# First layer's weights in three transfers, tails turned by four full transposes: a change at the two ends of a tuned kernel

## The chip, the cores and the metric

The kernel runs on one NeuronCore of a Trainium2 chip. The metric is device microseconds of one execution (lower is better). The time counted is about 1.8 us longer than the span that the profile shows.

Words used below: TensorE does the matmuls, and also turns (transposes) blocks, by a matmul with a unit matrix. Its results go to a buffer, PSUM, of which this kernel uses eight parts, the banks. ScalarE and VectorE copy them out, multiply and add. A transfer is issued by an engine's queue, is then carried out by the DMA engines, and has landed when its semaphore says so.

## The reference, cut to what matters

```python
B, F, D, L = 16384, 26, 16, 6            # Din = F * D = 416
def reference(x0, ws, bs):               # x0 [16384, 416], ws [6, 416, 416], bs [6, 416], bf16
    x = x0
    for l in range(L):
        proj = jnp.einsum('bd,de->be', x, ws[l]) + bs[l]
        x = x0 * proj + x
    return x
```

416 columns are three full tiles of 128 and a tail of 32. The kernel keeps the activations transposed (features on partitions) and cuts the batch into eight groups of 2048 rows, each of four chunks of 512.

## The kernel before: the parts that the change and the argument touch

The program records operations with what they read and write, and puts semaphore waits between them. Each `lane` is a semaphore of a transfer. The start of the SP queue (the SyncE queue that issues transfers), in program order:

```python
def load_wm(l, eng):                      # three full tiles of a layer's weights: one transfer, 312 KB
    add(eng, lambda h: h.dma_start(wm[l][:, :, :], ws[l, 0:NT * P, :].rearrange("(t p) f -> p t f", p=P)),
        writes=[("wm", l)], lane=f"wm{l}", batch=0)
...
load_nat(0, 0, 2); load_nat(0, 2, KK)     # group 0, chunk 0, row-major, 208 KB each
load_wm(0, "sp")
for j in range(1, NJ):                    # chunks 1 to 3
    load_nat(j, 0, 2); load_nat(j, 2, KK)
load_w3(0, "sp")                          # weights of the tail: four small transfers
load_group(1)                             # four DMA transposes of group 1, then four copies of its tails
```

Group 0 is turned by TensorE, group 1 by the DMA engines. `load_group` issues the transposes of tile 0, of the block that holds the tail, of tile 1 and of tile 2, and then the four tail copies.

The last layer of the last group is computed row-major, so that its result can be stored as it is. For that its input has to be turned: tiles 0 and 1 by DMA transposes, tile 2 and the tails by TensorE.

```python
def turn_tails(bks):                      # before: sixteen 32x32 transposes into four banks, one copy
    for kk in range(KK):
        for j in range(NJ):
            r, q = quad(g, l, j)
            add("pe", lambda h, ...: h.matmul(psum_t(b)[:, kk * T32:(kk + 1) * T32], x3col(j, kk), ident[q, q],
                is_transpose=True, tile_position=(r * T32, 0)), ..., writes=[("ps", bks[j])])
    add("act", lambda h: h.activation(x5n[:, :, :, NT * P:D], ..., ACT_F.Copy), reads=[("ps", b) for b in bks] + ...)
...
# rest_turn(1): issues on the SP queue, with a store between the two halves
#   transpose of chunks 0, 1 -> x5n ; store of part of the group before ; transpose of chunks 2, 3 -> x5n
# then, on VectorE:  nat_mul(0, 0), nat_mul(0, 2), nat_add(0, 0), nat_add(0, 2), nat_mul(1, 0) ...
```

`nat_add(0, 2)` is the first operation that needs the second half of that transpose.

## Time and profile before

| | kernel before |
|---|---|
| time, median of six runs | 476.96 us (476.26 to 477.49) |
| span of the profiled execution | 476.1 us |
| TensorE busy | 467.7 us, 98% |
| tail copies of group 1 landed and TensorE goes on | at 22.89 us |
| from there to the issue of the last transpose (460.91) | 438.02 us |
| that transpose, issue to landing | 5.35 us |

The profiled execution itself took 477.91 us. TensorE's timeline of the kernel before (start, length, engine, line, what, and in brackets the idle time and what ended it):

```profile
460.08 0.19 PE L850 MATMUL ps<-ident,x 32*128 32x32 bf16 x3
460.45 0.26 PE L850 MATMUL ps<-ident,x 32*128 32x32 bf16 x13 [0.17 <-ACT tw L395]
...
461.42 0.62 PE L832 MATMUL ps<-ident,x 128*128 128x128 bf16 x8 [0.35 <-ACT x L857]
```

The first two lines are the sixteen small transposes, split by a wait for ScalarE to leave the last of the four banks; the third is the turn of tile 2 (L832), which then waits until ScalarE has copied the tails out.

### The profile page before, as it was taken

What the parts mean: (1) busy time and instruction counts of PE and PEld (TensorE: products, weight loads), DVE (VectorE), ACT (ScalarE), POOL (GpSimd) and SP (SyncE); (2) the same over time, 40 slices, a digit from 0 to 9 for tenths busy, and PEclk for the clock granted to TensorE, in tenths of its full rate; (3) what the DMA queues carried; (4) which work ended last, traced back from release to release, by engine and by line L of the source; (5) the groups of instructions that cost most, each with busy time, mean ns of one, the idle gap of its engine ahead of it and who ended that gap; (6) DMA issues with size and microseconds to landing.
All of it is one profiled execution on the core that took longest, in us unless ns stands there. A gap on an engine that the chain in (4) does not pass through costs nothing.

```text
span 476.1 us, 8364 instructions
## 1 busy us (share of the span) xinstructions
PE 467.7 (98%) x3356; PEld 193.4 (41%) x3356; DVE 403.3 (85%) x695; ACT 341.7 (72%) x371; POOL 5.8 (1%) x15
## 2 busy tenths in 40 slices
PE   8899999999999999999999999999999999999995
PEld 5344444444444444444444444444444444444342
DVE  2788888888888888898889879888888888888886
ACT  4577777777777777777777777777777777777785
POOL 1000000000000000000000000000000000000000
PEclk9999999999999999999999999999999999999999
DMA  8966860630102397369318941980000039025898
GB/s 223 161 163 150 174 122 1 144 79 0 30 7 43 64 224 154 81 143 246 77 25 195 220 95 26 175 264 0 2 12 23 8 64 240 12 45 122 226 192 247
DMA packets 138859, 53.31 MB, mean 112 GB/s; under 512 B 112442, under 2 KB 138308, under 8 KB 138820
## 3 DMA queue, kind: packets, MB, share of 16 engines
q1 hardware_dynamic: 138664, 52.67, 49.6%
q8 instruction: 26, 0.43, 0.4%
q10 hardware_dynamic: 156, 0.11, 0.1%
q14 instruction: 13, 0.11, 0.1%
HBM read 5.97 MB, written 13.63 MB: 41 GB/s over the span
## 4 chain that ended last, share of the span: by engine, by line
PE 90%; SPq 4%; DVE 3%; DMA 2%; ACT 0%; issue 0%; DVEq 0%
PE ps L457 75%; PE ps L478 7%; PE ps L498 7%; SPq L292 2%; DMA x<-x 1%; PE ps L472 1%; DVE x L887 1%; SPq L522 1%; DVE x L881 1%; DVE x L409 1%; DVE tw L404 1%; PE ps L489 1%; SPq L297 0%; ACT tw L395 0%; DMA x<-ost 0%; SPq L303 0%
## 5 line engine op out<-in xcount | busy, mean ns | idle before, releaser
L395 ACT ACTIVATE tw<-ps,bias 128x1024 bf16<-128x1024 f32 (+1 forms) x295 | 299.6, 1070 | 121.4 <-PE ps L478 82.2
L457 PE MATMUL ps<-x,wm 128*128 128x512 bf16 x1692 | 379.6, 380 | 1.3 <-DMA x<-in_x_dram 0.8
L457 PEld LDWEIGHTS ps<-x,wm 128*128 128x128 bf16 x1692 | 158.7, 98 | 215.3 <-issue 28.2
L404 DVE TENSOR_TENSOR tw<-tw,x 128x1024 bf16<-128x1024 bf16 (+1 forms) x285 | 192.8, 684 | 55.6 <-ACT tw L395 55.2
L409 DVE TENSOR_TENSOR x<-tw,x 128x1024 bf16<-128x1024 bf16 (+1 forms) x285 | 182.5, 681 | 0.0
L478 PE MATMUL ps<-x,w 32*128 32x512 bf16 x512 | 39.2, 379 | 0.8 <-DMA x<-ost 0.8
L498 PE MATMUL ps<-x,wm 128*32 128x512 bf16 x564 | 33.0, 380 | 0.0
L435 ACT ACTIVATE ts<-ps,bias 128x512 bf16<-128x512 f32 x47 | 28.7, 700 | 0.0
L498 PEld LDWEIGHTS ps<-x,wm 128*32 128x32 bf16 x564 | 13.8, 96 | 17.6 <-issue 5.3
L439 DVE TENSOR_TENSOR x<-ts,x 128x512 bf16<-128x512 bf16 x47 | 18.6, 418 | 2.4 <-DMA x<-x 2.4
L478 PEld LDWEIGHTS ps<-x,w 32*128 32x128 bf16 x512 | 7.8, 92 | 28.5 <-issue 27.1
L437 DVE TENSOR_TENSOR ts<-ts,x 128x512 bf16<-128x512 bf16 x47 | 18.6, 418 | 0.0
L821 PE MATMUL ps<-wm,x 128*128 128x416 bf16 x48 | 9.5, 340 | 0.0
L684 POOL COPY ost<-ot 128x512 bf16<-128x512 bf16 x6 | 4.3, 720 | 423.7 <-DMA ot<-x 423.7
L875 ACT ACTIVATE x<-ps 128x416 bf16<-128x416 f32 x16 | 7.7, 534 | 2.0 <-PE ps L821 1.9
L575 DVE COPY x<-ps 128x512 bf16<-128x512 bf16 x5 | 2.0, 422 | 8.2 <-PE ps L565 8.1
L577 ACT ACTIVATE x<-ps 128x512 bf16<-128x512 bf16 x7 | 3.8, 595 | 4.9 <-PE ps L565 4.9
L821 PEld LDWEIGHTS ps<-wm,x 128*128 128x128 bf16 x48 | 4.3, 98 | 4.2 <-issue 1.0
L887 DVE TENSOR_TENSOR x<-x,x 128x832 bf16<-128x832 bf16 (+1 forms) x9 | 4.8, 542 | 1.4 <-DMA x<-x 1.3
L489 PE MATMUL ps<-x,w 32*32 32x512 bf16 x188 | 5.9, 374 | 0.0
L472 PE MATMUL ps<-x,w 32*32 32x512 bf16 x208 | 5.6, 385 | 0.0
L881 DVE TENSOR_TENSOR x<-x,x 128x832 bf16<-128x832 bf16 (+1 forms) x10 | 4.8, 500 | 0.7 <-ACT x L875 0.7
(40 smaller groups left out, 32.0 us busy)
## 6 DMA issues: line engine op xcount, KB each, us to landing
out_dram<-ost SPq DMA_DIRECT2D x6, 1664.0 KB, 7.2
x<-x SPq DMA_DIRECT2D x24, 96.0 KB, 2.1
wm<-in_ws_dram SPq DMA_DIRECT2D x6, 312.0 KB, 3.4
x<-in_x_dram SPq DMA_DIRECT2D x8, 208.0 KB, 4.2
x<-in_x_dram SPq DMA_DIRECT2D x4, 416.0 KB, 8.0
x<-x SPq DMA_DIRECT2D x22, 64.0 KB, 2.0
out_dram<-x SPq DMA_DIRECT2D x3, 416.0 KB, 3.6
x<-ost SPq DMA_DIRECT2D x28, 32.0 KB, 2.0
```

What stands on the lines that cost most here:

```text
L395: add("act", lambda h, a=a, w=w, b0=b0: h.activation(tw[r][:, a * CH:(a + w) * CH], psum[:, b0 * CH:(b0 + w) * CH], ACT_F.Identity, bias=b ...
L404: add("dve", lambda h, a=a, e=e: h.tensor_tensor(tw[r][:, a * CH:e * CH], tw[r][:, a * CH:e * CH], x0s[s0][:, i * GC + a * CH:i * GC + e * ...
L409: add("dve", lambda h, a=a, e=e: h.tensor_tensor(xs[so][:, i * GC + a * CH:i * GC + e * CH], tw[r][:, a * CH:e * CH], src(i, a, e), ALU.ad ...
L435: add("act", lambda h: h.activation(ts[r][:, :], bank(b), ACT_F.Identity, bias=bias[:, 3, l:l + 1], scale=1.0), reads=[("ps", b), "bias"], ...
L437: add("dve", lambda h: h.tensor_tensor(ts[r][:, :], ts[r][:, :], x03, ALU.mult), reads=[("ts", r)] + tok0, writes=[("ts", r)], release=True)
L439: add("dve", lambda h: h.tensor_tensor(x3s[so][:, :], ts[r][:, :], res, ALU.add), reads=[("ts", r)] + rtok, writes=[("x3", so), ("x3", so, ...
L457: add("pe", lambda h, t=t, j=j: h.matmul(bank(banks[j]), wm[l][:, t, ecols], src(t, j, j + 1), start=(first and t == 0), stop=(not first a ...
L472: add("pe", lambda h, q=q, j=j, r=r, c=c, o=o: h.matmul(psum[o, banks[j] * CH:(banks[j] + 1) * CH], w3[l][q, i * P + c * T32:i * P + (c + ...
L478: add("pe", lambda h, q=q, j=j, r=r: h.matmul(bank(banks[j]), w3[l][q, ecols], src[q, :], start=first, stop=not first, tile_position=(r * ...
L489: add("pe", lambda h, l=l, b=b, s3=s3, ri=ri, qi=qi, ro=ro, qo=qo: h.matmul(psum[qo, b * CH:(b + 1) * CH], w3[l][qi, NT * P:D], s3[qi, :], ...
L498: add("pe", lambda h, t=t, j=j, src=src, l=l, b=b, ro=ro, qo=qo: h.matmul(psum[qo, b * CH:(b + 1) * CH], wm[l][:, t, NT * P:D], src(t, j, ...
L821: add("pe", lambda h, t=t: h.matmul(bank(b, n=D), xcol(t, j, kk), wm[l][:, t, :], start=(first and t == 0), stop=(not first and t == NT - 1)),
```

## The change

Its intent: the first matmul needs only a third of the weights, so let it start when that third is there; and the tails need fewer, larger instructions, one bank and no wait for the others.

```diff
+    def wm_tok(l, t):
+        return ("wm", l) if l else ("wm", l, t)
+
+    def load_wm0(t):
+        add("sp", lambda h: h.dma_start(wm[0][:, t, :], ws[0, t * P:(t + 1) * P, :]),
+            writes=[wm_tok(0, t)], lane=f"wm0{t}", batch=0)
...
-    load_wm(0, "sp")
+    for t in range(NT):
+        load_wm0(t)
...
-    def turn_tails(bks):
+    def turn_tails(b):
+
         for kk in range(KK):
-            for j in range(NJ):
... (the sixteen transposes and the one copy go)
+            add("pe", lambda h, kk=kk: h.transpose(
+                psum_t(b)[:, kk * P:(kk + 1) * P], s3[:, kk * P:(kk + 1) * P], ident[:, :]),
+                reads=tok3 + ["ident"], writes=[("ps", b)])
+        sp_ = psum_t(b)[:, 0:KK * P].rearrange("p (k q f) -> p q k f", k=KK, q=NJ)
+        j = 0
+        while j < NJ:
+            r = quad(g, l, j)[0]
+            n = min(NJ - j, NJ - r)
+            add("act", lambda h, j=j, r=r, n=n: h.activation(
+                x5n[:, j:j + n, :, NT * P:D], sp_[:, r:r + n, :, :], ACT_F.Copy), ...)
+            j += n
...
-    turn_tails([b0, b1, b2, b3])
+    turn_tails(b0)
```

Matmuls that read the first layer's weights now depend on the third that they use.

More of the change, by code (lines that the diff above doesn't have):

```diff
@@ L280, in load_wm @@
         add(eng, lambda h: h.dma_start(wm[l][:, :, :], ws[l, 0:NT * P, :].rearrange("(t p) f -> p t f", p=P)),
-            writes=[("wm", l)], lane=f"wm{l}", batch=0)
+            writes=[wm_tok(l, t) for t in range(NT)], lane=f"wm{l}", batch=0)
+    def wm_tok(l, t):
[3 more added lines that the diff above has]
+            writes=[wm_tok(0, t)], lane=f"wm0{t}", batch=0)
     def load_w3(l, eng):
@@ L459, in full @@
                 start=(first and t == 0), stop=(not first and t == NT - 1)),
-                reads=[stok(t, j), ("wm", l)], writes=[("ps", banks[j])])
+                reads=[stok(t, j), wm_tok(l, t)], writes=[("ps", banks[j])])
             if after_chunk and t == NT - 1:
@@ L500, in tails @@
                         start=False, stop=(t == NT - 1), tile_position=(0, ro * T32)),
-                        reads=[stok(t, j), ("wm", l)], writes=[("ps", b)])
+                        reads=[stok(t, j), wm_tok(l, t)], writes=[("ps", b)])
             evacuate_tail(g, l, b)
@@ L823, in nat_full @@
                 stop=(not first and t == NT - 1)),
-                reads=[stok(t, j), ("wm", l)], writes=[("ps", b)])
+                reads=[stok(t, j), wm_tok(l, t)], writes=[("ps", b)])
     def turn_last(j, b):
@@ L844, in turned_out @@
             add("dve", lambda h: h.tensor_copy(dst, sp_), **kw)
-    def turn_tails(bks):
+    def turn_tails(b):
         for kk in range(KK):
-            for j in range(NJ):
-                r, q = quad(g, l, j)
-                add("pe", lambda h, b=bks[j], j=j, kk=kk, q=q, r=r: h.matmul(
-                    psum_t(b)[:, kk * T32:(kk + 1) * T32], x3col(j, kk), ident[q, q], is_transpose=True,
-                    tile_position=(r * T32, 0)),
-                    reads=tok3 + ["ident"], writes=[("ps", bks[j])])
-        b = bks[0]
-        assert bks == list(range(b, b + NJ))
-        sp_ = psum[:, b * CH:(b + NJ) * CH].bitcast(BF16).rearrange("p (j c) -> p j c", j=NJ)[:, :, 0:KK * T32]
-        add("act", lambda h: h.activation(
-            x5n[:, :, :, NT * P:D], sp_.rearrange("p j (k f) -> p j k f", k=KK), ACT_F.Copy),
-            reads=[("ps", b) for b in bks] + ["x5 free"], writes=[("x5n", j, NT) for j in range(NJ)])
+            add("pe", lambda h, kk=kk: h.transpose(
[7 more added lines that the diff above has]
+            add("act", lambda h, j=j, r=r, n=n: h.activation(
+                x5n[:, j:j + n, :, NT * P:D], sp_[:, r:r + n, :, :], ACT_F.Copy),
+                reads=[("ps", b), "x5 free"], writes=[("x5n", a, NT) for a in range(j, j + n)])
+            j += n
     def nat_rows(kk, bks, first=True):
```

## The prediction

> **What bounds the kernel now.** I read the page first: busy shares, then the chain that ended last.
>
> ```profile
> PE 467.7 (98%) x3356; PEld 193.4 (41%) x3356; DVE 403.3 (85%) x695; ACT 341.7 (72%) x371; POOL 5.8 (1%) x15
> PE 90%; SPq 4%; DVE 3%; DMA 2%; ACT 0%; issue 0%; DVEq 0%
> ```
>
> TensorE is busy 98% of 476.1 us and carries 90% of the chain. In the view of waits between 24 and 455 us no row names PE itself as waiting for data, so that middle part is a solid run of matmuls which the change doesn't touch. The change can only act at the two ends, where the chain isn't TensorE: the start (SPq, the queue that issues transfers, 4%) and the end (VectorE 3%, DMA 2%). So I read the timeline of each engine there.
>
> The start, first the transfer queue, then TensorE (columns: start us, length us, engine, line, what; in brackets the idle time before it and who ended it):
>
> ```profile
> 0.73 0.88 SPq L522 DMA_DIRECT2D x<-in_x_dram  x2
> 1.65 0.43 SPq L280 DMA_DIRECT2D wm<-in_ws_dram  x1
> 2.13 2.86 SPq L522 DMA_DIRECT2D x<-in_x_dram  x6
> 5.03 1.82 SPq L285 DMA_DIRECT2D w<-in_ws_dram  x4
> 6.89 3.68 SPq L292 DMA_TRANSPOSE x<-in_x_dram  x1
> 10.62 2.12 SPq L297 DMA_TRANSPOSE ost<-in_x_dram  x1
> 12.78 6.22 SPq L292 DMA_TRANSPOSE x<-in_x_dram  x2
> 19.04 2.51 SPq L303 DMA_DIRECT2D x<-ost  x4
> ```
>
> ```profile
> 5.82 1.46 PE L457 MATMUL ps<-x,wm 128*128 128x512 bf16 x6 [0.46 <-DMA wm<-in_ws_dram]
> ...
> 18.36 1.90 PE L457 MATMUL ps<-x,wm 128*128 128x512 bf16 x8
> 21.08 1.04 PE L457 MATMUL ps<-x,wm 128*128 128x512 bf16 x4 [0.82 <-DMA x<-in_x_dram]
> 22.89 0.61 PE L478 MATMUL ps<-x,w 32*128 32x512 bf16 x8 [0.77 <-DMA x<-ost]
> ```
>
> The reader should see that the queue never rests from 0.73 to 21.55 us: eight loads of the first batch group, the first layer's weights (L280) in between, small weights (L285), then four DMA transposes of the second group and four small copies of its tails. TensorE waits 0.46 us for the weights at 5.82, but later waits 0.82 us for the second group's last transpose and 0.77 us for its last tail copy. **Those two later waits set the start**: whatever TensorE gains before 20.26 us (the end of the stretch at 18.36) it only waits longer there. The chain says the same: it goes from the queue's issues through L292, L297 and L303 to the tail copy's landing and only then onto PE.
>
> The end, VectorE and the transfer queue:
>
> ```profile
> 464.54 0.59 DVE L887 TENSOR_TENSOR x<-x,x 128x832 bf16<-128x832 bf16 x1
> 466.38 0.59 DVE L887 TENSOR_TENSOR x<-x,x 128x832 bf16<-128x832 bf16 x1 [1.25 <-DMA x<-x]
> 466.89 0.58 DVE L881 TENSOR_TENSOR x<-x,x 128x832 bf16<-128x832 bf16 x1
> ```
>
> ```profile
> 458.89 1.34 SPq L705 DMA_TRANSPOSE x<-x  x1
> 460.40 0.45 SPq L691 DMA_DIRECT2D out_dram<-ost  x1
> 460.91 1.44 SPq L705 DMA_TRANSPOSE x<-x  x1
> ```
>
> VectorE sits idle 1.25 us until the transpose issued at 460.91 lands (5.35 us in the chain), and from 466.38 to 473.82 it runs back to back. So the end is set by that landing plus VectorE's last 7.4 us. TensorE's and ScalarE's work between 460 and 466 has slack.
>
> **What the Trainium skill says.** (1) "DMA: Bandwidth & Descriptors", section "Issuing engines are not separate DMA queues": all transfers share the same 16 engines and interleave; issuing from more places saves only the sequencer's time. Trace: one issue takes 0.43 us and repeats every 0.47 to 0.48 us, and from 2 to 9 us the DMA share is 0.82 to 1.10 in every 1 us window, so the engines are the scarce thing there. (2) "ScalarE: Activation LUTs", section "What ACT_TABLE_LOAD costs": an ACTIVATE with immediate operands takes 186 ns + 0.833 ns per element, and back-to-back ones overlap by about 93 ns. For 512 elements that is 612 ns; the trace's tail copy took 597 ns. It agrees. (3) "TensorE: Matmul & The Clock Gate", section "Back-to-back issue gap": weight load plus matmul pairs of 128 columns sustain about 81 ns each. Trace: eight 128x128 transposes (L832) took 0.62 us, 77 ns each.
>
> **The change, part by part.**
>
> *Weights in three transfers.* One 312 KB issue becomes three of 104 KB. Bytes are the same. The queue gets two more issues: 2 x 0.475 = **0.95 us**. Everything behind them (the six loads, small weights, the second group) is issued up to 0.95 us later. For it: before, the weights landed 4.0 us after the issue, at 5.65; the first third should land about 1 us sooner. The first matmul then waits for its transposed input instead: ScalarE's copies of chunk 0 end at 5.84, so TensorE can start a few tenths earlier at most. That is worth 0 because of the later waits.
>
> Can the first group's later arrival hurt? TensorE would reach the waits at most 0.95 us later, 21.21 instead of 20.26, and there is 0.82 + 0.77 = 1.59 us of waiting to swallow it. Not beyond the second group's own shift.
>
> How much of the 0.95 us reaches the second group? If the queue is the limit: all of it. If the DMA engines are: less. Evidence for the engines: a later transpose of the same size, at 87.02 us, was issued in 1.43 us, while the first one here took 3.68 and one at 169.90 took 7.35. So an issue stretches while older transfers drain. Likewise the small weight loads land 4.5 to 5.1 us after issue here, against a median of 2.3 over the run: some 2.5 us of work stood in front of them. With the two issues added, the same bytes drain at nearly the same time (pieces of 104 KB every 0.475 us are 0.22 MB/us, below the 0.24 to 0.38 MB/us that the windows show being moved, but two 208 KB loads stand in front as a buffer). Then the first transpose would be issued in less than 3.68 us and give some of the 0.95 back. Against: by 14.95 us one slice of 0.65 us shows no DMA work at all, so the engines aren't saturated throughout the transposes. I choose a bit over half: **+0.5 us** at 22.89, and from there one for one, as TensorE has no gap until 455 us.
>
> *Tails by four full transposes.* Removed: sixteen 32x32 transposes into four banks (0.19 + 0.26 us busy with a 0.17 us wait for ScalarE's last eviction between them) and one copy of 512 elements per partition (0.597 us). Added: four 128x128 transposes (4 x 77 ns = 0.31 us) and, as this layer's blocks are rotated by two, two copies of 256 elements. A copy of 1024 took 1.05 us, so the slope is (1.05 - 0.597)/512 = 0.885 ns per element; one of 256 is 0.597 - 0.227 = 0.37 us; two with 0.1 us overlap are 0.64 us, so +0.04 us on ScalarE. Moved: the tails need only one bank free, and the next transposes (L832) no longer wait for the copy, which ended at 461.37. They then wait for VectorE's add of chunk 1, ending at 460.97: about 0.4 us earlier than 461.42. The second L832 group still needs VectorE's adds of chunks 2 and 3, ending at 461.97, so it stays near 462.0. Off the chain, all of it: the add at 466.38 waits for a transfer whose issue at 460.91 the change doesn't move. **Worth 0.0 us** in time; the idle 1.25 us grows a little.
>
> Sum: 477.1 + 0.5 + 0.0 = **477.6 us**.
>
> **Rivals.** *Full pass-through*: the queue is the limit, +0.95, 478.05. For it: the chain runs through the queue's issues; against it: the stretched issue times. *Absorbed*: the engines are the limit, 477.1 to 477.3. *The intended gain*: the 0.46 us wait at the start and 0.4 us at the tail come off, 476.3 to 476.7. Against it: both lie in front of a longer wait for another transfer. *A new wait at the end*: two copies instead of one delay ScalarE's evictions and so VectorE. They'd have to slip by more than 1.25 us; the estimate is 0.04.
>
> **Range and chances.** The two middle rivals span 477.1 to 478.05; noise of the kernel before is 477.0 to 477.49. I take 477.0 to 478.2. 2% is 9.5 us, and all effects named are under 1 us: faster 0.005, same 0.985, slower 0.01.
>
> **What would show it.** Right: three L280 issues from 1.65 on and the first transpose issued near 7.84 rather than 6.89; its issue shorter than 3.68 us; the tail copy's wait at 22.89 ending 0.2 to 1.0 us later; between there and 455 us the same length; L832 starting 0.3 to 0.4 us earlier relative to the last tile, and VectorE still waiting for the transfer before its second L887, then back to back. Wrong: if the wait at 22.89 ends at the same time or sooner, the queue's issues were fully hidden; if the stretch from 461 us to the end shortens, the tail was on the chain and the wait for the transfer depended on it; if the middle changes length, something I have not seen.

## The result, and the profile after

The changed kernel took **477.7 us** (477.6 to 478.06, six runs) against 476.96 for the kernel before: a ratio of 1.0018, interval 1.0005 to 1.0031. Ratios are the mean time of one kernel's runs over that of the other's runs of the same rounds, so not quite the ratio of the medians. In microseconds the ratio is 0.0018 x 477 = +0.9. So it is within 2%, and slightly slower.

The profiled execution hardly shows it: its span is 476.2 us against 476.1. The SP queue of the changed kernel at the start:

```profile
1.65 1.77 SPq L287 DMA_DIRECT2D wm<-in_ws_dram  x3
3.46 2.81 SPq L529 DMA_DIRECT2D x<-in_x_dram  x6
6.31 1.82 SPq L292 DMA_DIRECT2D w<-in_ws_dram  x4
8.18 2.60 SPq L299 DMA_TRANSPOSE x<-in_x_dram  x1
10.83 3.46 SPq L304 DMA_TRANSPOSE ost<-in_x_dram  x1
14.34 4.53 SPq L299 DMA_TRANSPOSE x<-in_x_dram  x2
18.91 2.52 SPq L310 DMA_DIRECT2D x<-ost  x4
```

Set this beside the same view in the prediction. The three weight issues take 1.77 us together (two of them 0.43 us, one 0.83), where the single one took 0.43, so the first transpose is issued 1.29 us later (8.18 for 6.89). But its own issue takes 2.60 us instead of 3.68, and the tail copies start at 18.91, a little sooner than before's 19.04. TensorE of the changed kernel:

```profile
5.73 1.86 PE L464 MATMUL ps<-x,wm 128*128 128x512 bf16 x6
...
21.34 1.04 PE L464 MATMUL ps<-x,wm 128*128 128x512 bf16 x4 [0.48 <-DMA x<-in_x_dram]
22.76 0.61 PE L485 MATMUL ps<-x,w 32*128 32x512 bf16 x8 [0.39 <-DMA x<-ost]
```

The wait for the weights at 5.82 is gone, and it is worth nothing, as TensorE waits later for the second group. In this one execution that later wait ends at 22.76, 0.13 us sooner than in the one before. One pair of traces thus says that the two issues were hidden, while the times say otherwise. The profiled executions took 477.91 us (before) and 478.02 us (after), so this pair differs far less than the medians do; the experiments have to settle it.

The end. TensorE and VectorE of the changed kernel, two views:

```profile
459.86 0.39 PE L857 MATMUL ps<-ident,x 128*128 128x128 bf16 x4
...
460.64 0.65 PE L840 MATMUL ps<-ident,x 128*128 128x128 bf16 x8
```

```profile
463.98 0.59 DVE L896 TENSOR_TENSOR x<-x,x 128x832 bf16<-128x832 bf16 x1
466.47 0.59 DVE L896 TENSOR_TENSOR x<-x,x 128x832 bf16<-128x832 bf16 x1 [1.90 <-DMA x<-x]
466.98 0.58 DVE L890 TENSOR_TENSOR x<-x,x 128x832 bf16<-128x832 bf16 x1
```

The four full transposes take 0.39 us with no wait, and the turn of tile 2 starts at 460.64 instead of 461.42. VectorE now idles 1.90 us instead of 1.25 before its second add: what was gained is waited away. The landing that it waits for comes later, too. The chain of the two kernels, at that transfer (start, length, what), first before, then after:

```profile
460.91 5.35 DMA x<-x
```

```profile
460.77 5.58 DMA x<-x
```

### The profile page after: what moved, and what is told of

It reads as the page before. It is cut to its first block, busy times and chain, and to the rows that moved or that the text cites. A ratio compares the mean times of both kernels' runs of the same rounds, so it can differ in the third digit from the quotient of the medians.

```text
span 476.2 us, 8290 instructions
## 1 busy us (share of the span) xinstructions
PE 463.2 (97%) x3290; PEld 193.8 (41%) x3344; DVE 403.4 (85%) x695; ACT 342.2 (72%) x372; POOL 6.1 (1%) x15
## 4 chain that ended last, share of the span: by engine, by line
PE 88%; SPq 4%; DVE 3%; DMA 2%; issue 1%; ACT 1%; DVEq 0%
PE ps L464 74%; PE ps L485 7%; PE ps L505 6%; SPq L299 1%; ACT tw L402 1%; DMA x<-x 1%; PE ps L479 1%; DVE x L896 1%; SPq L304 1%; SPq L529 1%; DVE x L890 1%; DVE x L416 1%; DVE tw L411 1%; PE ps L496 0%; DMA x<-ost 0%
## 5 line engine op out<-in xcount | busy, mean ns | idle before, releaser
L464 PE MATMUL ps<-x,wm 128*128 128x512 bf16 x1638 | 372.5, 380 | 6.1 <-issue 3.7
```

The costliest lines, as they stand in the source:

```text
L464: add("pe", lambda h, t=t, j=j: h.matmul(bank(banks[j]), wm[l][:, t, ecols], src(t, j, j + 1), start=(first and t == 0), stop=(not first a ...
```

## The experiments

Theory 1 is the prediction's: at the start the queue passes on about half of its extra issues (+0.5 us for two), and the tails are off the chain. Rival A: the DMA engines are the limit and swallow the issues. Rival B: all of it is passed on. Rival C: the tails cost something at the end. All kernels gave correct results. The kernel before ran in the same rounds of each set of four.

The table holds, from each run's trace, when the first transpose of group 1 was issued, when the issues of all four were over, when TensorE went on with that group's tails, and how long the last transpose at the end took to land, as the chain has it; then the time ratio. The first two rows are the traces already shown.

| run | first issued | four issued by | TensorE goes on | last lands after | span | ratio to before (95%) |
|---|---|---|---|---|---|---|
| before | 6.89 | 19.00 | 22.89 | 5.35 | 476.1 | |
| after | 8.18 | 18.87 | 22.76 | 5.58 | 476.2 | 1.0018 (1.0005 to 1.0031) |
| n1 before again | 6.90 | 18.90 | 22.79 | 5.36 | 476.0 | 1.0000 (0.9988 to 1.0013) |
| n2 start only | 8.10 | 19.58 | 23.48 | 5.32 | 476.6 | 1.0005 (0.9992 to 1.0019) |
| n9 start only | 8.15 | 19.06 | 22.95 | 5.42 | 476.2 | 1.0006 (0.9994 to 1.0018) |
| n10 two small more | 7.84 | 19.85 | 23.75 | 5.32 | 476.9 | 1.0015 (1.0002 to 1.0028) |
| n5 six transfers | 9.21 | 18.99 | 23.32 | 5.33 | 476.5 | 1.0029 (1.0012 to 1.0046) |
| n6 weights on ScalarE's queue | 4.51 | 17.24 | 21.14 | 5.38 | 474.4 | 0.9974 (0.9959 to 0.9989) |
| n12 change, on ScalarE's queue | 4.75 | 18.33 | 22.60 | 5.54 | 476.0 | 1.0024 (1.0008 to 1.0040) |
| n3 tails only | 7.24 | 18.65 | 22.55 | 5.55 | 475.9 | 1.0003 (0.9990 to 1.0017) |
| n11 tails only | 7.30 | 17.83 | 21.72 | 4.21 | 474.6 | 1.0004 (0.9990 to 1.0019) |
| n7 tails, all banks | 7.25 | 18.46 | 22.36 | 5.57 | 475.8 | 0.9993 (0.9980 to 1.0007) |
| n8 slack at the end used | 7.14 | 18.65 | 22.56 | | 475.6 | 1.0002 (0.9987 to 1.0017) |
| n4 after again | 8.19 | 18.74 | 22.63 | 5.53 | 476.0 | 1.0013 (1.0001 to 1.0026) |

**n1, the kernel before itself**, unchanged.

> The kernel before itself, as a control. Every theory expects the ratio 1.000 with an interval of about 0.002; its profile on this chip shows how far the landing of the tail copy (22.89 us in the first profile), the length of the middle and the landing of the last transpose (466.26) move from one execution to the next when nothing is changed.

The ratio was 1.0000. Single runs of this kernel on this chip went from 476.52 to 477.83 us, so the effects sought, of half a microsecond, lie inside the spread of single runs. The middle is rigid: from 22.79 to the issue of the last transpose at 460.81 is 438.02 us. In every trace of the table but n8's, where that issue was moved, this distance is 438.00 to 438.02 us. So what differs between executions arises in the first 23 us or the last 15.

**n2 and n9, the start alone** (the changed kernel with the old `turn_tails`).

```diff
-    turn_tails(b0)
+    turn_tails([b0, b1, b2, b3])     # and the old body
```

> Only the weights in three transfers. Theory 1 (the queue passes on about half of its two extra issues): +0.5 us, and the wait for the tail copy ends 0.2 to 1.0 us later. Rival A (the DMA engines are the limit at the start and swallow it all): 0.0 us, the wait ends within 0.2 us of the control's. Rival B (full pass-through): +0.95 us.

> Only the weights in three transfers, measured again for a tighter interval. The first time gave a ratio of 1.0005 (0.9992 to 1.0019). If two extra issues cost what five fewer saved and five more cost, about 0.25 us each: +0.5 us. If they are swallowed: 0.0 us.

They gave +0.2 and +0.3 us (ratios 1.0005 and 1.0006). Both intervals hold 0 and 0.5, and both end at 0.9 us, below the 1.04 us by which the queue was late (next lines). So the times speak against full pass-through, and leave open whether the start alone costs anything. The traces tell a little more. Six traces have the old start (before, n1, n3, n7, n8, n11): the first transpose was issued at 7.12 us in the mean, and TensorE went on at 22.48. Four have the split start (after, n2, n4, n9): 8.16 and 22.96. So 1.04 us later at the queue became **0.48 us** later at TensorE. In the means that is half, as Theory 1 had it. But the old starts alone spread from 21.72 to 22.89, which is why the first pair of traces misled: the before of that pair was the latest of the six. From the spread within the two sets (standard deviations of 0.42 and 0.37), the standard error of the 0.48 is about 0.25, so it is a likely size, not a proven one. Two warnings go with it. A trace is one run and need not be a typical one: in n1, n2, n3, n9 and n10 it was the slowest run of its kernel's set, in n5 and n11 the fastest. And within each set the table's order is the reverse of a delay passed on: the later the first transpose was issued, the sooner all four were over (old starts from 6.89 and 19.00 down to 7.30 and 17.83; split starts from 8.10 and 19.58 down to 8.19 and 18.74). So no fixed share is shown, and why the starts vary this way stays open.

**n10, two small transfers instead of the split.**

```diff
     load_wm(0, "sp")
+    for t in range(2):
+        add("sp", lambda h, t=t: h.dma_start(scrap[:, t * 8:(t + 1) * 8], ws[0, 0:P, 0:8]),
+            writes=[("scrap", t)], lane=f"scrap{t}", batch=0)
```

> Weights whole in one transfer, old tails, and two tiny transfers (16 bytes a partition) to a scratch tile in the place of the two extra issues. If the issues on the queue are what costs: +0.5 us, as the split. If it is that the weights travel in smaller pieces or on three semaphores: 0.0 us.

+0.7 us (ratio 1.0015, clear of 1), with the weights whole and the old tails. So two issues on the queue at this place cost by themselves; it takes neither smaller pieces of the weights nor a wait for three semaphores. SP queue, then TensorE, of n10:

```profile
2.13 0.96 SPq L534 DMA_DIRECT2D scrap<-in_ws_dram  x2
...
7.84 2.29 SPq L293 DMA_TRANSPOSE x<-in_x_dram  x1
```

```profile
22.03 1.04 PE L458 MATMUL ps<-x,wm 128*128 128x512 bf16 x4 [1.01 <-DMA x<-in_x_dram]
23.75 0.61 PE L479 MATMUL ps<-x,w 32*128 32x512 bf16 x8 [0.69 <-DMA x<-ost]
```

The first transpose again is issued in less time (2.29 us), and yet both waits for group 1 end later than in any of the six old starts. (This trace is the slowest of five runs.)

**n5, six transfers** (old tails, each third again cut in two by columns).

```diff
+        for c in (0, 1):
+            cs = slice(c * D // 2, (c + 1) * D // 2)
+            add("sp", lambda h, cs=cs: h.dma_start(wm[0][:, t, cs], ws[0, t * P:(t + 1) * P, cs]), ...)
```

> The weights in six transfers (same bytes), old tails: five extra issues on the queue in place of two, about 2.4 to 3.0 us before the second group. Theory 1 as predicted (half is passed on): +1.2 to 1.5 us. Rival A (the DMA engines swallow the issues as long as they have older transfers to drain): no more than +0.6 us, because the second group's transposes are then issued in less time. Rival B (full pass-through): +2.4 us or more.

+1.4 us (0.0029 x 477), the size that Theory 1 gave, but not quite by its mechanism. TensorE of n5:

```profile
9.74 1.16 PE L575 MATMUL ps<-ident,x 128*128 128x128 bf16 x12 [1.44 <-DMA x<-in_x_dram]
...
20.62 2.76 PE L466 MATMUL ps<-x,wm 128*128 128x512 bf16 x12
23.32 0.61 PE L487 MATMUL ps<-x,w 32*128 32x512 bf16 x8
```

TensorE waits 1.44 us at 9.74 for the first group's chunk 1, reaches group 1 only at 20.62, and doesn't wait for it at all. Group 1's issues were over at 18.99, only 0.4 us later than the 18.58 mean of the six old starts. So with five extra issues the *first* group's late arrival is the limit. Its loads were issued late, from 4.49 us instead of 2.13, and not slow: from issue to landing they took 3.5 us in the median, against 4.2 in the kernel before. There is a second path behind the one that two issues lengthen. One thing is not separated here: the six pieces also have rows half as long (208 columns).

**n6, the first layer's weights issued by ScalarE's queue** (weights whole, old tails).

```diff
+    load_wm(0, "act")                # ahead of ScalarE's table load
...
+    load_w3(0, "act")                # behind it
-    load_wm(0, "sp")
-    load_w3(0, "sp")
```

> Old tails, weights whole, but the first layer's five weight transfers are issued by ScalarE's queue: five issues fewer on the SP queue, so the second group's first transpose is issued about 2.4 us sooner. Rival A (engines are the limit): 0.0 to -0.4 us, the first transpose's own issue gets longer, up to 5 us. Rival B and theory 1 (queue is the limit, wholly or by half): -0.8 to -1.6 us, the latter being all that TensorE waits there.

-1.24 us (ratio 0.9974), clear of 1: **this version beats both kernels.** SP queue, then TensorE, of n6:

```profile
0.73 3.73 SPq L522 DMA_DIRECT2D x<-in_x_dram  x8
4.51 4.46 SPq L292 DMA_TRANSPOSE x<-in_x_dram  x1
...
17.28 2.51 SPq L303 DMA_DIRECT2D x<-ost  x4
```

```profile
5.19 1.52 PE L457 MATMUL ps<-x,wm 128*128 128x512 bf16 x6
...
18.42 2.76 PE L457 MATMUL ps<-x,wm 128*128 128x512 bf16 x12
21.14 0.61 PE L478 MATMUL ps<-x,w 32*128 32x512 bf16 x8
```

The transposes start 2.6 us before the mean of the old starts and are over 1.3 us before it: again about half. The first one's issue stretches to 4.46 us, presumably because the first group's loads still drain. No wait for group 1 is left, so its transposes are no longer the limit: issues taken away in front of them alone could not help further. The matmuls also begin sooner (5.19 us for 5.82); how much of the gain that allows is not separated.

**n12, the whole change with its transfers on ScalarE's queue.**

```diff
-        add("sp", lambda h: h.dma_start(wm[0][:, t, :], ...
+        add("act", lambda h: h.dma_start(wm[0][:, t, :], ...
```

(and the three loads and `load_w3` moved to where n6 has them)

> The whole change, but the first layer's weights, in their three transfers, and its four small weight transfers go out on ScalarE's queue. If the change's cost is its issues on the SP queue: as fast as the run with whole weights on ScalarE's queue (ratio 0.9974), within 0.3 us, so -0.9 to -1.5 us. If the split or the tails cost by themselves: 0.5 us or more above that.

A miss: +1.1 us (ratio 1.0024) where I had expected n6's gain. The mean hides two groups: three of the six runs took 477.5 to 477.8 us (the kernel before's median here was 477.38) and three 479.2 to 479.8. In either group n6's gain is gone. The trace is of the first group. TensorE of n12:

```profile
6.87 0.38 PE L464 MATMUL ps<-x,wm 128*128 128x512 bf16 x1 [0.58 <-DMA wm<-in_ws_dram]
7.80 1.02 PE L464 MATMUL ps<-x,wm 128*128 128x512 bf16 x4 [0.55 <-DMA wm<-in_ws_dram]
...
19.91 2.76 PE L464 MATMUL ps<-x,wm 128*128 128x512 bf16 x12
22.60 0.61 PE L485 MATMUL ps<-x,w 32*128 32x512 bf16 x8
```

The second and third pieces of the weights arrive last. They landed up to 5.5 us after their issue, where the whole weights of n6 took 3.5 and the three pieces of the changed kernel on the SP queue at most 3.1. With the queue free of them, the eight loads of the first group follow each other at once, and it is likely that they compete with the pieces: the loads too took longer from issue to landing, 5.5 us in the median, against 4.9 in n6 and 3.7 in the changed kernel. The two more issues also hold up ScalarE's own work, whose first copies start at 5.05 us instead of n6's 4.54. TensorE starts its stream late and never waits for group 1. So the sentence "only the issues on the SP queue cost" is wrong for the split: beside a dense stream of loads, the pieces themselves came late. Of the three slower runs there is no trace. Their granted clock is 0.994, that of the other three 0.996 to 0.998. Whether this is the cause stays open: runs of the changed kernel at 0.997 and at 1.000 had the same span, 475.8 us.

**n3 and n11, the tails alone** (the kernel before with the new `turn_tails`).

```diff
-    turn_tails([b0, b1, b2, b3])
+    turn_tails(b0)                   # and the new body
```

> Only the four full transposes of the tails. Theory 1 (the tail work is off the chain): 0.0 us within 0.2, with VectorE's idle time before its second add longer by 0.3 to 0.6 us. Rival C (the earlier TensorE and ScalarE work shifts the last transpose's landing, or the two copies cost time on the chain): +0.2 us or more, with the landing of the last transpose later against its issue than in the control (5.35 us in the first profile, 5.58 in the changed kernel's).

> Only the new tails, measured again. The last transpose should again land 5.5 to 5.6 us after its issue, against 5.3 to 5.4 with the old tails. Time: +0.2 us if that is passed on to the end, 0.0 if not.

Time: +0.15 and +0.2 us by ratios of 1.0003 and 1.0004, not told from zero. In n3 VectorE idled 1.89 us before its second add, 0.64 us longer than in the kernel before. In n3 the last transpose landed 5.55 us after its issue. Of the traces with the new tails and the old order of issues, five are alike (5.53, 5.54, 5.55, 5.57, 5.58); all seven with the old tails have 5.32 to 5.42. But n11, the same kernel as n3, had 4.21, against my expectation. So 0.2 us later is usual with the new tails, not a law.

Where it happens, it is passed on to the end. As the middle is rigid, count from TensorE's start on group 1's tails to the start of VectorE's last line. In the seven traces with the old tails this is 450.24 to 450.34 us, in the five alike with the new ones 450.43 to 450.50: **+0.2 us**, with no overlap. That is Rival C, small as it is, and far sharper than the times. n11 had 449.14, so its VectorE was done 1.3 us sooner than n3's; but from the same starting point to the end of the span it took 452.9 us against n3's 453.4, only 0.5 us less (n8 below shows why).

What the transfers do in that time does differ. DMA throughput from 456 to 472 us, in slices of 0.4 us (busy tenths, then GB/s), before and then n3:

```profile
DMA  9913998999799999999990008999999999999998
GB/s 283 289 28 74 216 213 156 190 214 191 158 216 204 242 360 287 315 209 209 253 132 0 7 10 295 343 333 331 333 333 329 337 327 327 339 327 327 339 318 250
```

```profile
DMA  9319998997999999999999999999959950099920
GB/s 284 60 41 219 210 174 175 212 195 148 215 205 219 363 287 343 204 214 211 265 380 324 312 324 331 329 333 335 268 198 352 354 183 21 21 318 354 349 60 6
```

With the old tails the engines move next to nothing for three slices (0, 7 and 10 GB/s, from 464.4 to 465.6 us), and the awaited transpose lands after that pause. With the new ones the stores flow on without it, and the landing, behind them, still is no earlier. It is the same in every trace: the seven with the old tails have three such slices (14 GB/s at most) before the landing, the seven with the new tails have none there. That the pause goes and the landing mostly doesn't move forward is shown; why is not.

**n7, the new tails made to wait for all four banks**, and to hold them, as the old ones did.

```diff
-                reads=tok3 + ["ident"], writes=[("ps", b)])
+                reads=tok3 + ["ident"], writes=[("ps", x) for x in bks])
```

(and the copies read all four)

> The new tails alone, but made to wait for all four banks and to hold them, as the old ones did, so that the work after them runs as late as before. In three traces with the new tails the last transpose landed 5.53 to 5.58 us after its issue, in three with the old 5.32 to 5.36. If the earlier work of TensorE, VectorE and ScalarE beside the transfer causes those 0.2 us: about 5.35 here. If the form of the new transposes and copies causes them: 5.55 here. Time: within 0.3 us of the kernel before in either case.

VectorE idled 1.31 us before its second add, as in the kernel before, and the landing took 5.57 us. So the later landing is not caused by the earlier compute beside it: that was taken away and the landing stayed. The pause is absent here too, so it goes with the new form of the turns and copies, not with their being early. Since n11 shows 4.21 with the same four transposes, I don't name the cause beyond that. The time (0.9993) is the same as before's within the interval.

**n8, the slack at the end put to use** (new tails, old start).

```diff
-            if t and j0:
-                store(LAST - 1, 0, 1)            # now behind both halves of the transpose
...
-    for j in (0, 2):
-        nat_add(0, j)
-    nat_store(0, 0, NJ)
+    nat_add(0, 0)                                # nat_mul(1, 0) now comes before nat_add(0, 2)
```

> The new tails, and the slack before the last landing put to use: the second half of that transpose is issued ahead of a store that stood before it (0.5 us sooner), and VectorE does the next row block's first multiply (0.5 us) before the add that waits for it. Old start. If the end is set by that landing and VectorE's run after it, as the traces say: -0.8 to -1.1 us. If the end is set by something else, ScalarE's evictions for instance: 0.0 to -0.4 us.

A miss in time: ratio 1.0002. Yet VectorE did what was hoped. Its last line in n8, and in n3 (same start within 0.01 us, at 22.56 and 22.55):

```profile
471.67 0.65 DVE L888 TENSOR_TENSOR x<-x,x 128x416 bf16<-128x416 bf16 x2
```

```profile
473.02 0.65 DVE L888 TENSOR_TENSOR x<-x,x 128x416 bf16<-128x416 bf16 x2
```

The work ends 1.35 us sooner, and the span is shorter by only 0.3 us (475.6 for 475.9). The rest is waited for by the SP queue, which holds the program open until the last stores have landed. Waits of the SP queue at the end, in the kernel before and in n8 (line, what it waited for, us in total, times, longest):

```profile
SPq L180 <- DMA out_dram<-x: 1.6, 3, 1.0
```

```profile
SPq L180 <- DMA out_dram<-x: 2.6, 3, 2.1
```

The last stores of n8 land 2.8 us after their issue instead of 1.7 to 1.8. It is not that the engines are full: in slices of 0.1 us they move 267 GB/s at 473.5 us and then only 8 to 50 until 474.6, while n3's are at 150 to 358 GB/s from 474.3 until 475.0 us and are then done. So the bulk of the stores did end earlier, but a thin rest took most of the gain; n11, whose landing came early, has the same rest (17 to 42 GB/s from 472.8 to 473.5 us). "The landing plus VectorE's last run" is the limit only until it is shortened; the last stores stand right behind it. Why their rest is slow is not shown.

**n4, the whole change again.**

> The whole change again on this chip, beside its parts. Theory 1: +0.5 us (0.3 to 1.0), the sum of the two parts. If the parts do not add up to it, there is an interaction.

+0.6 us (ratio 1.0013, interval 0.05 to 1.2 us). The parts, +0.2 to +0.3 us for the start and +0.2 for the tails by the times (0.48 and 0.2 by the traces), add up to 0.4 to 0.7, so no interaction is needed to explain it.

## Why the prediction was right

The time, 477.7 us, was foreseen as 477.6, and the range held it. That number alone decides little, and its closeness is partly luck: full absorption (477.1 to 477.3) and full pass-through (478.05) lay in the range too, and the sum began at 477.1, the median of three runs, where six gave 476.96. The rise was foreseen as +0.5 and measured as +0.9 and +0.6.

- **The start, +0.5 us: the direction is shown, the half is only likely.** That issues in front of the second group cost time is shown by n10 (two tiny transfers, +0.7 us) and n6 (five fewer, -1.24), both clear of 1; in n5 (+1.4) the cost came by way of the first group. That not all of it is passed on, as the first transpose is then mostly issued in less time (2.41 to 2.60 us in the four split starts, 2.17 to 3.77 in the six old ones), fits the intervals of n2 and n9, which end below the full 1.04. The share of a half is 0.48 us with a standard error of 0.25, and the times of the start alone (+0.2 and +0.3) are not told from zero. The delay of the queue itself was mis-sized: 1.29 us in the first pair instead of 0.95, because one of the three issues took 0.83 us, not 0.43. (A small misreading: the four small weight loads landed 4.5 to 5.2 us after their issue, not 4.5 to 5.1.)
- **The test that I named for it was wrong.** The prediction says that a wait ending at the same time or sooner would mean that the issues were fully hidden. It ended 0.13 us sooner in the first pair, and the issues weren't hidden: one execution's start lies anywhere in 1.2 us. Even ten traces give the half microsecond only with the error named above.
- **The first group's later arrival "can't hurt": right for two issues, and the reason held.** In all four split starts TensorE still waits for group 1's tails, 0.29 to 0.73 us. With five it does hurt (n5), as the delay then exceeds the waiting that swallows it.
- **The earlier first matmul is worth nothing: right.** The 0.46 us wait is gone and TensorE waits later instead.
- **The tails, 0.0 us: mis-sized by 0.2 us.** The prediction called them off the chain, because the add waits for a transfer "whose issue at 460.91 the change doesn't move". The issue indeed doesn't move, but the landing does: it came 5.53 to 5.58 us after the issue instead of 5.32 to 5.42 in five of six traces, and VectorE's last line moved by the same 0.2 us. The times of the tails alone (1.0003, 1.0004 and, all banks, 0.9993) can't tell this from zero. ScalarE's two copies took 0.66 us against 0.64 foreseen; the four transposes 0.39 against 0.31. The step to the next transposes was mis-sized too: measured against the issue of the last transpose, their first group (L832 in before, L840 in after) started 0.64 us earlier, not 0.3 to 0.4, because it had begun before VectorE's add of chunk 1 ended, for which I had made it wait. The second group, foreseen to stay near 462.0, started at 461.57.
- **The end is set by that landing and VectorE's run after it: right for these two kernels**, as VectorE runs back to back from it in both, but narrower than it sounds: n8 by its edit and n11 by its early landing shortened that path by over a microsecond, and the final stores took most of it back.
- **The middle keeps its length: right**, to 0.02 us.

Left open: what share of the queue's delay is passed on, why the landing comes later with the new tails (and did not in n11), the pause of the DMA engines, and n12's slower runs.

## What to carry to other kernels

A transfer that is cut into pieces costs issues on its queue, and whatever stands behind them in that queue can pay; look at what is last in the queue before looking at what the first piece frees, and at which later wait the freed time would fall into. Moving whole transfers to an idle queue can gain more than cutting them, but see that the pieces don't then lose against the loads that now flow unhindered. And where effects are half a microsecond and the start varies by more than one, compare sets of traces, at a point behind which everything is rigid.

## What the Trainium skill lacked or had wrong

- "DMA: Bandwidth & Descriptors", section "Issuing engines are not separate DMA queues", calls the time that a sequencer saves by issuing elsewhere "usually small relative to the DMA itself". Here five issues moved from the SP queue to ScalarE's took 1.24 us off the run (ratio 0.9974), since two waits of TensorE hung on the queue's last issues. It also says that the transfers interleave, but not what that can cost small ones: the pieces of n12 landed up to 5.5 us after their issue, at most 3.1 in the changed kernel.
- No page that I read gives, for this chip, the time for which issuing a DMA transpose of this size holds the SP queue, or says how much it varies: 1.43 to 7.35 us for the same size within one trace of the kernel before, and 2.17 to 5.13 us for the first one of the start over all runs.
- No page that I read has the pause in which the 16 engines moved 0, 7 and 10 GB/s in three slices of 0.4 us, with a transpose in flight and stores behind it; all seven traces with the old tails have it.
- "TensorE: Matmul & The Clock Gate", section "Back-to-back issue gap", gives about 81 ns for a 128-column pair. Counted from a group's first start to the start of what follows it, four of these transposes took 0.32 us (80 ns each), but eight took 0.49 us (61 ns each) in the changed kernel, and 24 at the start of the kernel before took 1.36 us (57 ns each, from 7.11 to 8.47): longer runs of transposes go faster than the page's figure.
- Nothing wrong in "ScalarE: Activation LUTs", section "What ACT_TABLE_LOAD costs": by its numbers two copies of 256 elements take 2 x 399 - 93 = 705 ns, an estimate; they took 660.
